# Gated linear attention and maxout FFN on one core: weights' conversion with one step less, joined output sums, turns' sums in four column tiles, and all lists written anew

## The chip, the core and the metric

One core of one Trainium2 chip runs the kernel. Its engines are TensorE (PE; the profile calls its weight loads PEld), VectorE (DVE), ScalarE (ACT), GpSimd (POOL) and SyncE (SP), which here only starts transfers. The metric is the device time of one execution in microseconds, the median of several runs.

## The reference

Two blocks follow each other. The first is a gated linear recurrence over 768 steps, for 4 batches of 8 heads with 48 features. The second is a maxout FFN over the 3072 tokens, from 384 features to 768 and back.

```python
mag = np.sqrt(a_re * a_re + a_im * a_im)
scale = np.minimum(mag, 0.999) / (mag + 1e-06)
a_re_n, a_im_n = (a_re * scale, a_im * scale)
for t in range(S):
    ar, ai = (a_re_n[:, :, t, :, None], a_im_n[:, :, t, :, None])
    new_re = ar * S_re - ai * S_im
    new_im = ar * S_im + ai * S_re
    kv = np.einsum('bhd,bhe->bhde', k[:, :, t], v[:, :, t])
    S_re, S_im = (new_re + kv, new_im)
    y[:, :, t] = np.einsum('bhd,bhde->bhe', q[:, :, t], S_re)
...
x = np.ascontiguousarray(attn_out.transpose(0, 2, 1, 3)).reshape(B * S, H * D)
h = np.maximum(np.maximum(x @ w1, x @ w2), x @ w3)
return (h @ w_out).astype(np.float32)
```

The four FFN weights arrive as 64-bit floats; all else is float32.

## The kernel before

**Tiling.** The tokens are cut into 12 groups, numbered 0 to 11; a group holds 128 steps of two batches, called x and y. The recurrence is computed by chunks: per group the gates' magnitude and angle, the sums of their logarithms and angles along the steps, and with these products inside a chunk and a state carried to the next.

**The list of words.** All work is written as words "name:group" in one string, SCHEDULE (line 21); `run` (line 955) does them one after the other. A last letter x or y names the batch, a 0 or 1 the batch in the early words of group 0. Each engine is wrapped in `Bound` (line 201), which ties each instruction behind the one issued before it on the same engine. So an engine works strictly in the order of the list, and waits where a word's inputs are not there. Because every call goes through `Bound`, all instructions bear its line, 210, in the profile. SLOTS (line 127) says which of four PSUM buffers of two banks each product gets; OTHER (line 134) names the words that run on the alternative engine, mostly DVE in place of ACT.

**The words that matter here.**

- `sqr`, `sqi`, `add`, `lnL`, `expe`, `expw`, `relu`, `lne`, `abs`, `xor`, `half`, `stt`, `atan`, `turn` turn the gates into logarithms (tiles Ln, L) and angles (tile w), on ACT and DVE.
- `cs` (line 586) sums the angles along the steps by a product with a triangle of ones, `upto`; per batch four matmuls, each with 64 columns of `upto`, so that two of them fill the array's columns. `t`, `nf`, `af`, `sa`, `sb` round the sums and take sine and cosine. `sums`, `F` and the `E` words do the like for the logarithms.
- `mk`, `mq`, `uk`, `uq` scale k and q (tiles k, q, uk, uq); `tpk`, `tpq` transpose them on PE into PSUM tile tp, and `Kc`, `Qc` copy that to tiles K and Q.
- `A` and `B` are the scores inside a chunk, `dk` the state's increment, `h` words carry the state (tile g), `y` is the block's output and `x` copies it to the FFN's features (tile xhx; xT in group 0). A, B and y use 32 columns of the array per matmul; sums, tp, dk and F use 64; the FFN's products use the whole array.
- `U` is the product with 768 x 384 blocks of a weight (PSUM tile up) and `u` the relu (first weight, folded into the others by `T`, `M`, `Wg`) or the running maximum. In group 0 they have shorter forms, and `O`, `o` are its output product.
- From group 1 on, the output product goes by seven half-size products, `P1` to `P7`, with `Px`, `Py` (PSUM tile op), and sums `S1` to `S4` (tile strassen) before and `r1`, `r6`, `r5`, `r7`, `r57`, `ox`, `oy` behind, which gather the result in tile ot. `D` stores it.
- `WL` loads one of 12 blocks of the weights as pairs of 32-bit words. `weight_step` (line 431) converts it to float32 into its place (tiles w and wo) through a scratch tile `ex` that lies in xhx: step `a` on ACT, `b`, `c`, `e`, `f` on DVE. The words of a pair are `low` and `high`, views that read every second word. The words are Wa, Wb and so on.

The loaded and intermediate tiles of the attention block come from pools with two buffers (`ldx`, `nat2`, `un2`, `fp2`).

Of the kernel before, what the change touches and what calls it, by code (L numbers as in the profile page):

```python
# [13 lines left out]
I32 = mybir.dt.int32  # L14
# [19 lines left out]
Bx:0 b0x:0 turn:1 b1x:0 h2x:0 mqx:1 Fx:1 f0x:1 We4:0 f1x:1 Wf4:0 f2x:1 add:2 csx:1 tx:1 yx:0 KBy:0 Q2y:0 nfx:1 xx:0
h3x:0 f3x:1 lnL:2 expe:2 Q1y:0 WL5:0 Wa5:0 Lkx:1 sumsy:1 csy:1 Eky:1 ty:1 Ay:0 kEny:0 Wb5:0 WL7:0 relu:2 mkx:1
g0y:0 Wc5:0 expw:2 U01x:0 nfy:1 abs:2 u01x:0 Lvy:1 We5:0 Eqy:1 Z2:0 g1y:0 Wa7:0 QBy:0 afy:1 Wf5:0 Eny:1 g2y:0 g3y:0
Wb7:0 Wg4:0 U11x:0 xor:2 By:0 dky:0 U02x:0 Lvx:1 b1y:0 h1y:0 b0y:0 QGy:0 yy:0 addw:2 lnw:2 expL:2 xy:0 U11y:0 Wg5:0
u02x:0 U02y:0 afx:1 half:2 u11x:0 Wc7:0 lne:2 We7:0 mulw:2 mulai:2 sbx:1 h2y:0 Z4:0 sax:1 h3y:0 stt:2 atan:2 Wf7:0
U12x:0 u12x:0 say:1 sby:1 Cdy:1 WL8:0 Cdx:1 turn:2 ukx:1 uqx:1 U01y:0 u01y:0 u11y:0 Wa8:0 U12y:0 csy:2 ty:2 u12y:0
csx:2 tpqx:1 tx:2 u02y:0 Qcx:1 nfy:2 Lnop:2 nfx:2 tpkx:1 Fy:1 kEnx:1 Wb8:0 Wc8:0 We8:0 Kcx:1 Wg7:0 Wf8:0 U21y:0  # L40
Wg8:0 KBx:1 f0y:1 u21y:0 Lky:1 Lqy:1 mky:1 afy:2 sumsx:2 dkx:1 Q1x:1 f1y:1 f2y:1 f3y:1 Enx:2 U21x:0 u21x:0 afx:2
U22y:0 u22y:0 Oy:0 Lqx:2 mqy:1 uky:1 uqy:1 tpqy:1 Ekx:2 Lix:3 Q2x:1 say:2 sby:2 sbx:2 sax:2 Eqx:2 h0x:1 h1x:1 QGx:1
h2x:1 oy:0 QBx:1 mkx:2 h3x:1 Qcy:1 Q1y:1 tpky:1 Kcy:1 Ax:1 g0x:1 Q2y:1 Liy:3 sqi:3 Fx:2 sumsy:2 g1x:1 g2x:1 U22x:0
Lrx:3 u22x:0 g3x:1 f3x:2 f2x:2 f1x:2 f0x:2 Lry:3 sqr:3 add:3 lnL:3 expe:3 Ay:1 relu:3 J3:0 g0y:1 g1y:1 mqx:2 g2y:1
Bx:1 KBy:1 kEny:1 lne:3 Ox:0 Eky:2 b1x:1 Eny:2 QBy:1 b0x:1 h0y:1 ukx:2 By:1 Eqy:2 yx:1 g3y:1 xx:1 b1y:1 Lqy:2 mqy:2
Lvx:2 ox:0 Lky:2 mky:2 b0y:1 tpkx:2 expw:3 Kcx:2 uqx:2 Lnop:3 uqy:2 tpqx:2 Qcx:2 QGy:1 dky:1 h1y:1 kEnx:2 sumsx:3
uky:2 Ekx:3 h2y:1 Eqx:3 Enx:3 yy:1 xy:1 Fy:2 f3y:2 h3y:1 dkx:2 f2y:2 abs:3 KBx:2 h0x:2 h1x:2 Q1x:2 f0y:2 f1y:2
U11:1 u11:1 tpky:2 Kcy:2 Lky:3 QBx:2 QGx:2 addw:3 Lqx:3 h2x:2 mqx:3 h3x:2 xor:3 half:3 Cdx:2 tpqy:2 Qcy:2 Q2x:2
lnw:3 kEny:2 expL:3 sumsy:3 Eqy:3 Q2y:2 Eny:3 Lkx:3 mkx:3 Fx:3 Eky:3 U01:1 Ax:2 Q1y:2 J1:0 mulw:3 mulai:3 g0x:2
g1x:2 u01:1 Cdy:2 f3x:3 f2x:3 g2x:2 g3x:2 J2:0 Bx:2 f0x:3 Dx:0 f1x:3 Dy:0 stt:3 KBy:2 h0x:3 U12:1 b0x:2 b1x:2 u12:1  # L50
S3:1 Lvy:2 yx:2 U02:1 QBy:2 Lvx:3 Lry:4 atan:3 turn:3 Liy:4 csy:3 csx:3 Lix:4 Lrx:4 sqr:4 sqi:4 add:4 lnL:4 ty:3
xx:2 By:2 u02:1 Ay:2 S1:1 nfy:3 relu:4 tx:3 expe:4 S2:1 expw:4 P5:1 P6:1 g0y:2 afy:3 say:3 sby:3 nfx:3 sbx:3 g1y:2
afx:3 sax:3 abs:4 dky:2 P1:1 Lqy:3 g2y:2 g3y:2 b1y:2 J4:0 QGy:2 P7:1 Px:1 P2:1 b0y:2 h0y:2 h1y:2 ukx:3 tpkx:3 lne:4
Lnop:4 r1:1 Liy:5 mky:3 h2y:2 h3y:2 S4:1 Kcx:3 uqx:3 yy:2 Lqx:4 kEnx:3 mqy:3 tpqx:3 Qcx:3 P3:1 r6:1 xy:2 Py:1 r5:1
r7:1 P4:1 Fy:3 uky:3 r57:1 f0y:3 f1y:3 xor:4 half:4 oy:1 ox:1 Q1x:3 addw:4 dkx:3 h1x:3 Lvy:3 f2y:3 f3y:3 h0y:3
h2x:3 sumsx:4 Ekx:4 h3x:3 lnw:4 QGx:3 expL:4 Eqx:4 Fx:4 KBx:3 U11:2 Dx:1 QBx:3 mulai:4 Q2x:3 f2x:4 Enx:4 u11:2
Cdy:3 Lkx:4 f1x:4 f0x:4 U01:2 uqy:3 f3x:4 mulw:4 stt:4 atan:4 tpky:3 Kcy:3 Ax:3 g0x:3 mqx:4 g1x:3 Bx:3 g2x:3 g3x:3
b1x:3 b0x:3 u01:2 Cdx:3 turn:4 U02:2 Lrx:5 u02:2 mkx:4 kEny:3 csy:4 csx:4 tx:4 nfx:4 ty:4 nfy:4 yx:3 xx:3 sumsy:4
KBy:3 Eqy:4 Eky:4 Lry:5 S3:2 Eny:4 sqr:5 dky:3 h1y:3 h2y:3 h3y:3 tpqy:3 Qcy:3 Q2y:3 Lix:5 sqi:5 Px:2 afy:4 add:5
lnL:5 expe:5 Dy:1 U12:2 u12:2 S1:2 Py:2 P7:2 Q1y:3 relu:5 lne:5 QBy:3 afx:4 P4:2 Ay:3 By:3 expw:5 S2:2 g0y:3 sbx:4  # L60
abs:5 g1y:3 sax:4 QGy:3 ukx:4 uqx:4 P6:2 P5:2 S4:2 g2y:3 g3y:3 P2:2 P1:2 Lqy:4 r1:2 Liy:6 mqy:4 b1y:3 P3:2 b0y:3
r6:2 r5:2 r7:2 tpkx:4 r57:2 ox:2 oy:2 kEnx:4 tpqx:4 yy:3 xy:3 Fy:4 say:4 Lky:4 sby:4 mky:4 uky:4 Lnop:5 Kcx:4 uqy:4
sumsx:5 xor:5 half:5 U11:3 KBx:4 addw:5 lnw:5 expL:5 mulw:5 Lqx:5 mulai:5 Cdx:4 h0x:4 f2y:4 stt:5 f3y:4 Ekx:5 f0y:4
Lkx:5 Dy:2 Dx:2 Qcx:4 Enx:5 Q1x:4 Cdy:4 u11:3 Eqx:5 QBx:4 mkx:5 Lry:6 QGx:4 Lvx:4 U01:3 Lix:6 atan:5 Q2x:4 u01:3
f1y:4 h0y:4 U02:3 Lrx:6 u02:3 sqr:6 dkx:4 h1x:4 sqi:6 h2x:4 h3x:4 Fx:5 f0x:5 f3x:5 add:6 f1x:5 f2x:5 Ax:4 g0x:4
Lqy:5 g1x:4 Bx:4 lnL:6 expe:6 g2x:4 g3x:4 U12:3 lne:6 b1x:4 tpky:4 turn:5 mqx:5 b0x:4 tpqy:4 Qcy:4 u12:3 Lvy:4
kEny:4 S1:3 csy:5 ty:5 csx:5 Kcy:4 dky:4 nfy:5 S3:3 sumsy:5 h1y:4 h2y:4 tx:5 nfx:5 h3y:4 afy:5 yx:4 Eky:5 Eny:5
Eqy:5 afx:5 Q2y:4 Q1y:4 sbx:5 P5:3 P1:3 P7:3 Lky:5 sax:5 Ay:4 xx:4 KBy:4 ukx:5 uqx:5 Lrx:7 tpqx:5 S2:3 expw:6
relu:6 QBy:4 Lnop:6 mky:5 tpkx:5 S4:3 Kcx:5 g0y:4 Qcx:5 P6:3 Px:3 Py:3 r1:3 By:4 P2:3 P4:3 say:5 sby:5 QGy:4 g1y:4
abs:6 g2y:4 g3y:4 b1y:4 b0y:4 KBx:5 mqy:5 r6:3 r5:3 r7:3 r57:3 kEnx:5 oy:3 Q1x:5 uky:5 xor:6 Lry:7 sqr:7 Fy:5 f2y:5  # L70
sumsx:6 uqy:5 f3y:5 yy:4 P3:3 ox:3 f0y:5 Lkx:6 xy:4 QGx:5 addw:6 U11:4 Liy:7 Dx:3 QBx:5 Ekx:6 mkx:6 Enx:6 Lvx:5
f1y:5 lnw:6 Lqx:6 h0y:5 u11:4 Q2x:5 expL:6 mulai:6 mulw:6 U01:4 u01:4 tpky:5 h0x:5 Eqx:6 Kcy:5 tpqy:5 stt:6 Ax:5
Lix:7 atan:6 g0x:5 Qcy:5 g1x:5 g2x:5 Bx:5 kEny:5 g3x:5 b0x:5 Q2y:5 U02:4 sqi:7 b1x:5 add:7 lnL:7 relu:7 expe:7
u02:4 U12:4 Fx:6 f2x:6 S3:4 f3x:6 half:6 turn:6 f0x:6 u12:4 Lvy:5 dky:5 h1y:5 Q1y:5 f1x:6 sumsy:6 dkx:5 Eny:6 csy:6
csx:6 h1x:5 mqx:6 S1:4 Dy:3 ty:6 nfy:6 S2:4 Eqy:6 Lqy:6 mqy:6 Eky:6 P1:4 KBy:5 tx:6 nfx:6 afx:6 lne:7 expw:7 afy:6
P7:4 abs:7 Lky:6 Ay:5 QBy:5 g0y:5 g1y:5 g2y:5 yx:5 g3y:5 addw:7 sbx:6 sax:6 ukx:6 uqx:6 By:5 say:6 P5:4 xx:5 P6:4
r1:4 r6:4 r5:4 lnw:7 xor:7 S4:4 half:7 Px:4 P2:4 b0y:5 Py:4 r7:4 P4:4 r57:4 P3:4 expL:7 mulw:7 QGy:5 oy:4 tpqx:6
tpkx:6 b1y:5 Lnop:7 mky:6 Qcx:6 Q1x:6 ox:4 Liy:8 kEnx:6 yy:5 sumsx:7 xy:5 Cdx:6 Enx:7 Fy:6 f2y:6 f0y:6 f3y:6
mulai:7 f1y:6 Eqx:7 QBx:6 QGx:6 Q2x:6 stt:7 Lqx:7 Ekx:7 Lix:8 U01:5 sqi:8 Lry:8 Cdy:6 Kcx:6 Lrx:8 Lvx:6 dkx:6 h1x:6
sby:6 mqx:7 h2x:6 h3x:6 uqy:6 uky:6 sqr:8 add:8 Dy:4 atan:7 turn:7 Ax:6 g0x:6 lnL:8 Lkx:7 expe:8 xor:8 g1x:6 relu:8  # L80
# [962 lines left out]
```

## Time and profile before

| what | value |
|---|---|
| runs | 558.76, 561.72, 562.83 us; median 561.72 us |
| span of the profiled execution | 556.9 us |
| mean granted clock of TensorE | 0.988 |
| first matmul of PE | after 10.46 us |
| instructions | 22739 |

The profile is of one execution, and the span goes from its first instruction to its last; the time of a run holds in addition what lies around that, so the median is 4.8 us above the span. Busy times are sums over an engine's instructions. Matmuls overlap each other, so the mean duration of a matmul is longer than the step from one to the next.

### The profile page before, as it was taken

The page shows a single profiled execution, that of the slowest core. Times are in us where ns is not written, and L with a number is a line of the kernel's source. Part 1 is how long each engine was busy: PE and PEld are TensorE (multiplying, and loading weights), DVE is VectorE, ACT ScalarE, POOL GpSimd, SP SyncE. Part 2 cuts the span into 40 slices and gives each one's busy share as a digit, 9 for nine tenths or more (in the row PEclk, how much of TensorE's full clock was granted, in tenths as well). Part 3 has the DMA queues.
Part 4 walks back from the last instruction along what each step waited for, and adds up shares of the span by engine and source line. Part 5 has one row for each costly group of instructions (what it writes and reads, how often), then busy time and mean ns, then how long its engine had stood idle before and what let it go on. Part 6 is the DMA issues. An engine that isn't in the chain of part 4 may idle for free.

```text
span 556.9 us, 22739 instructions
## 1 busy us (share of the span) xinstructions
PE 524.6 (94%) x10086; PEld 449.0 (81%) x10086; DVE 490.4 (88%) x770; ACT 370.0 (66%) x652; POOL 74.4 (13%) x117
## 2 busy tenths in 40 slices
PE   1669799989999999999999999999999999999997
PEld 0356588778888898888988888988888888998986
DVE  5999999989998899999988897999999999886524
ACT  5999989867965867787766858777646855530100
POOL 8105250002030001000120200120010020000000
PEclk9869999999999999999999999999999999999999
DMA  8977976456055164235364136542361144000000
GB/s 218 287 191 156 206 154 102 78 105 123 18 108 109 21 123 77 48 63 92 68 115 82 33 61 121 110 88 50 58 126 31 32 88 82 10 31 2 7 25 29
DMA packets 142530, 49.09 MB, mean 88 GB/s; under 512 B 130528, under 2 KB 135648, under 8 KB 142432
## 3 DMA queue, kind: packets, MB, share of 16 engines
q1 hardware_dynamic: 136272, 37.77, 31.9%
q0 software_dynamic: 6160, 9.87, 10.4%
q8 instruction: 79, 1.29, 1.0%
q14 instruction: 19, 0.16, 0.1%
HBM read 33.03 MB, written 4.72 MB: 68 GB/s over the span
## 4 chain that ended last, share of the span: by engine, by line
PE 84%; DVE 6%; DMA 4%; SPq 2%; issue 1%; ACT 1%; POOL 0%; DVEq 0%
PE up L210 34%; PE op L210 24%; PE y L210 7%; PE A L210 5%; PE tp L210 4%; PE dk L210 4%; PE sums L210 3%; PE cs L210 2%; SPq L210 2%; DMA xhx<-in_moe_w_out_dram 2%; PE F L210 2%; DVE xhx L210 1%; PE B L210 1%; DMA k<-in_k_dram 1%; DMA ar<-nf 1%
## 5 line engine op out<-in xcount | busy, mean ns | idle before, releaser
L210 PE MATMUL up<-xhx,w 128*128 128x256 f32 x792 | 177.4, 382 | 0.1
L210 PEld LDWEIGHTS up<-xhx,w 128*128 128x128 f32 x792 | 148.6, 190 | 21.5 <-PE B L210 0.3
L210 ACT ACT_TABLE_LOAD x45 | 57.7, 1283 | 1.5 <-PEq L1027 0.8
L210 ACT COPY atm<-B 32x128 f32<-32x128 f32 x96 | 24.5, 255 | 36.9 <-DVE atm L210 22.9
L210 PE MATMUL op<-wo,xhx 128*128 128x192 f32 (+1 forms) x220 | 48.5, 364 | 0.0
L210 DVE TENSOR_TENSOR Q<-Q,f 112x1024 f32<-112x1024 f32 (+1 forms) x48 | 45.4, 950 | 0.8 <-ACT Q L210 0.6
L210 ACT ACTIVATE f<-F 48x232 f32<-48x232 f32 x96 | 34.4, 359 | 13.2 <-PE F L210 5.4
L210 POOL DMA_DIRECT2D ar<-nf x40 | 34.2, 1280 | 65.3 <-DVE ar L210 54.7
L210 PE MATMUL y<-atm,vb 128*32 128x64 f32 x1152 | 39.4, 221 | 1.4 <-issue 1.1
L210 PEld LDWEIGHTS op<-wo,xhx 128*128 128x128 f32 x220 | 36.5, 190 | 4.3 <-DVE q L210 0.3
L210 POOL DMA_DIRECT2D Ln<-e x11 | 11.1, 1005 | 214.6 <-ACT e L210 53.9
L210 PE MATMUL y<-QG,g 112*32 112x64 f32 x1408 | 38.4, 219 | 0.9 <-issue 0.8
L210 PEld LDWEIGHTS y<-atm,vb 128*32 128x32 f32 x1152 | 32.5, 109 | 6.4 <-issue 3.6
L210 PEld LDWEIGHTS y<-QG,g 112*32 112x32 f32 x1408 | 34.8, 109 | 1.3 <-issue 1.0
L210 DVE TENSOR_TENSOR ot<-ot,op 128x192 f32<-128x192 f32 (+1 forms) x67 | 27.1, 413 | 9.0 <-PE op L210 4.3
L210 PE MATMUL op<-wo,strassen 128*128 128x192 f32 x176 | 33.0, 331 | 0.0
L210 PE MATMUL A<-Q,K 112*32 112x80 f32 x1536 | 31.6, 234 | 1.3 <-DVE Q L210 1.3
L210 DVE COPY_PREDICATED atm<-masko,A 128x256 f32<-128x256 uint8 x72 | 31.2, 435 | 1.6
L210 PE MATMUL op<-w,strassen 128*128 128x192 f32 x176 | 32.5, 329 | 0.0
L210 PEld LDWEIGHTS A<-Q,K 112*32 112x32 f32 x1536 | 27.2, 110 | 5.0 <-issue 1.9
L210 ACT COPY Q<-tp 112x1024 f32<-112x1024 f32 x23 | 23.3, 1013 | 10.3 <-PE tp L210 10.0
L210 ACT COPY ot<-op 128x192 f32<-128x192 f32 (+1 forms) x13 | 4.5, 342 | 38.2 <-PE op L210 38.2
(151 smaller groups left out, 1120.8 us busy)
## 6 DMA issues: line engine op xcount, KB each, us to landing
ar<-in_a_re_dram SPq DMA_DIRECT2D x24, 192.0 KB, 3.7
ai<-in_a_im_dram SPq DMA_DIRECT2D x24, 192.0 KB, 3.8
q<-in_q_dram SPq DMA_DIRECT2D x96, 48.0 KB, 2.6
k<-in_k_dram SPq DMA_DIRECT2D x96, 48.0 KB, 2.9
vb<-in_v_dram SPq DMA_DIRECT2D x96, 48.0 KB, 3.1
out_dram<-ot SPq DMA_DIRECT2D x23, 192.0 KB, 2.8
Ln<-e POOLq DMA_DIRECT2D x11, 384.0 KB, 4.7
w<-L POOLq DMA_DIRECT2D x9, 384.0 KB, 4.7
```

Of the source, the lines that this page charges most:

```text
L210: ins = f(*a, **kw)
```

## The change

The diff has six parts.

1. **Weights' conversion.** The sign is kept through the conversion: step b now clips `high` from both sides and writes the scratch tile, a scales it in place with a function that treats the signs differently, c shifts, and e joins the low bits and writes the weight's place. Step f goes, and the sign bit is no longer masked and put back. The order is b, a, c, e.
2. **Output sums.** r5 and r7 become one addition, r75, over the middle half of a joined tile for both batches.
3. **Turns' sums in quarters.** `cs` makes eight matmuls of 32 columns in place of four of 64, per batch.
4. **Constants.** Biases of ACT are given as numbers and no longer read from tile `biases`, which keeps one column of ones.
5. **Fixed tiles.** The pools `ldx`, `nat2`, `un2`, `fp2` go; k, q, t, nf, af, CS, Ln, E, K, Q and ot are fixed tiles, one for each batch or for odd and even groups. Ek and Eq get tiles of their own.
6. **Lists.** SCHEDULE, SLOTS and OTHER are all new. The whole-array products are spread otherwise over the list. Among the words of OTHER (on DVE): Qc six times, before once; Kc four, before seven; the relu of u ten, before six; af eleven, before eight; x three, before five; relu of the logarithms three, before four.

```diff
-        if step == "a":
-            activation(out=ex.bitcast(FP), in_=high.bitcast(FP), func=AF.Abs, scale=2.0 ** -112)
-        elif step == "b":
-            dve.tensor_single_scalar(out=ex.bitcast(FP), in_=ex.bitcast(FP), scalar=LAST, op=OP.min)
+        if step == "b":
+            dve.tensor_scalar(out=ex.bitcast(FP), in0=high.bitcast(FP), scalar1=LAST, scalar2=-LAST, op0=OP.min,
+                              op1=OP.max)
+        elif step == "a":
+            activation(out=ex.bitcast(FP), in_=ex.bitcast(FP), func=AF.Prelu, alpha=-2.0 ** 32,
+                       scale=-2.0 ** -112 if i in (0, 3, 6) else 2.0 ** -112)
         elif step == "c":
-            if i in (0, 3, 6):
-                dve.tensor_scalar(out=ex, in0=ex, scalar1=3, scalar2=-0x80000000, op0=OP.logical_shift_left,
-                                  op1=OP.bitwise_or)
-            else:
-                dve.tensor_single_scalar(out=ex, in_=ex, scalar=3, op=OP.logical_shift_left)
+            dve.tensor_single_scalar(out=ex, in_=ex, scalar=3, op=OP.logical_shift_left)
         elif step == "e":
-            dve.scalar_tensor_tensor(out=ex, in0=low, scalar=29, in1=ex, op0=OP.logical_shift_right, op1=OP.bitwise_or)
-        elif step == "f":
-            dve.scalar_tensor_tensor(out=dst.bitcast(I32), in0=high, scalar=-0x80000000, in1=ex,
-                                     op0=OP.bitwise_and, op1=OP.bitwise_xor)
+            dve.scalar_tensor_tensor(out=dst.bitcast(I32), in0=low, scalar=29, in1=ex, op0=OP.logical_shift_right,
+                                     op1=OP.bitwise_or)
...
             for ch in range(2):
-                for j in range(2):
-                    dst, m = ps[j * L64:(j + 1) * L64, ch * HC:(ch + 1) * HC], slice(ch * L64, (ch + 1) * L64)
-                    mm(out=dst, lhsT=upto[:, m], rhs=every(T["w", g][:, c * DM:(c + 1) * DM], j), start=True, stop=True)
+                for o in (0, L64, 32, L64 + 32):
+                    j, m = o // L64, slice(ch * L64 + o % L64, ch * L64 + o % L64 + 32)
+                    mm(out=ps[o:o + 32, ch * HC:(ch + 1) * HC], lhsT=upto[:, m],
+                       rhs=every(T["w", g][:, c * DM:(c + 1) * DM], j), start=True, stop=True)
...
-                activation(out=e, in_=e, func=AF.Ln, scale=1e-6 * math.exp(-LNMAX), bias=least)
+                activation(out=e, in_=e, func=AF.Ln, scale=1e-6 * math.exp(-LNMAX), bias=math.exp(-LNMAX))
...
-                out, in0, in1 = {"r6": (yl, xl, r.get(6)), "r5": (xr, yl, r.get(5)), "r7": (yl, yl, r.get(7)),
-                                 "r57": (yr, yl, r.get(5)), "ox": (ot[0], ot[0], ps[:, 0, 0:DM]),
-                                 "oy": (ot[1], ot[1], ps[:, 1, 0:DM])}[name]
+                if name == "r75":
+                    two_ = ot.rearrange("p c n -> p (c n)")[:, NH:3 * NH].rearrange("p (u n) -> p u n", u=2)
+                    again = yl.rearrange("p (u n) -> p u n", u=1).to_broadcast([P, 2, NH])
+                    dve.tensor_tensor(out=two_, in0=again, in1=ps[:, 1, 0:DM].rearrange("p (u n) -> p u n", u=2), op=OP.add)
+                    return
+                out, in0, in1 = {"r6": (yl, xl, r.get(6)), "r57": (yr, yl, r.get(5)),
+                                 "ox": (ot[:, 0], ot[:, 0], ps[:, 0, 0:DM]),
+                                 "oy": (ot[:, 1], ot[:, 1], ps[:, 1, 0:DM])}[name]
```

More of the change, by code (lines that the diff above doesn't have):

```diff
@@ L62 @@
[L62 to L66, printed above, removed]
@@ L72 @@
[L72 to L76, printed above, removed]
@@ L77 @@
[L77 to L80, printed above, removed]
-g2x:6 mkx:7 U11:5 KBx:6 u11:5 g3x:6 U12:5 u01:5 lne:8 U02:5 u12:5 S3:5 Lnop:8 u02:5 Bx:6 b0x:6 b1x:6 tpky:6 tpqy:6
@@ L922, in seven @@
         else:
-            ot = [once(("ot", g * C + c), lambda: fp2.tile([P, DM], FP, tag="ot", name="ot")) for c in range(C)]
-            xl, xr, yl, yr = (ot[c][:, h * NH:(h + 1) * NH] for c in range(C) for h in range(2))
+            ot = ots
+            xl, xr, yl, yr = (ot[:, c, h * NH:(h + 1) * NH] for c in range(C) for h in range(2))
             if name == "r1":
```

254 lines of the change are left out of this document (133 added, 121 removed).

## The prediction

> **What bounds the kernel now.** I read the page first, then the busy time by stretches, then what TensorE (PE) waited for, then single rows.
>
> ```profile
> span 556.9 us, 22739 instructions
> ...
> PE 524.6 (94%) x10086; PEld 449.0 (81%) x10086; DVE 490.4 (88%) x770; ACT 370.0 (66%) x652; POOL 74.4 (13%) x117
> ...
> q8 instruction: 79, 1.29, 1.0%
> ...
> PE 84%; DVE 6%; DMA 4%; SPq 2%; issue 1%; ACT 1%; POOL 0%; DVEq 0%
> ```
>
> PE is busy 94% of the span and makes up 84% of the chain that ended last. DVE, at 88%, is close behind. The average hides two stages, which the stretches show:
>
> ```profile
> 20.00:40.00 20.00, 10.83 (x112) 7.62 (x104) 19.93 (x31) 19.80 (x33) 0.00 (x0) 0.66 0.88 220
> 40.00:60.00 20.00, 19.35 (x283) 12.19 (x282) 19.93 (x30) 18.92 (x28) 10.40 (x13) 1.00 0.79 169
> 60.00:80.00 20.00, 16.12 (x415) 13.78 (x416) 19.86 (x32) 18.06 (x37) 7.54 (x9) 1.00 0.89 182
> 90.00:557.00 467.00, 460.60 (x9032) 402.85 (x9024) 407.69 (x636) 290.51 (x514) 40.91 (x49) 1.00 0.35 67
> ```
>
> The columns are the stretch, its length, the busy time of PE, PEld, DVE, ACT and POOL, the granted clock, the DMA share and GB/s. From 20 to 80 us DVE works 19.9 of every 20 us and PE has gaps: this stage converts the weights and starts group 0, and DVE sets its end. From 90 us on PE works 460.60 of 467 us, the 6.4 us left containing the last add and store: here only PE's own time counts, and DVE has 59 us to spare. The waits of PE agree:
>
> ```profile
> PE pw L210 <- ACT w L210: 10.5, 1, 10.5
> PE cs L210 <- DVE w L210: 4.5, 2, 3.2
> PE tp L210 <- DVE uq L210: 2.6, 3, 1.7
> PE y L210 <- issue: 1.9, 2, 1.1
> ```
>
> The first three lie almost wholly in the first 90 us. The fourth, time in which PE waited for nothing that the profile shows, lies in the dense part. So three things can move the end: how far PE is behind its own work when it becomes dense, PE's own time after that, and these "issue" stalls.
>
> **PE's own time: changes of tile shape.**
>
> ```profile
> 143.72 1.52 PE L210 MATMUL cs<-w,upto 128*64 128x192 f32 x16
> 145.17 0.46 PE L210 MATMUL B<-QB,KB 112*32 112x32 f32 x32
> 145.44 1.33 PE L210 MATMUL A<-Q,K 112*32 112x80 f32 x64
> 146.71 0.43 PE L210 MATMUL op<-wo,strassen 128*128 128x192 f32 x1
> ```
>
> ```profile
> L210 PE MATMUL A<-Q,K 112*32 112x80 f32 x1216 | 25.0, 234 | 0.0
> ...
> L210 PE MATMUL cs<-w,upto 128*64 128x192 f32 x144 | 13.7, 332 | 0.0
> ...
> L210 PE MATMUL B<-QB,KB 112*32 112x32 f32 x608 | 8.9, 198 | 0.0
> ```
>
> A merged row ends one matmul's duration after its last start. The last cs began at 143.72 + 1.52 - 0.332 = 144.91. The 16 go in pairs (two column tiles of 64 at once), so a pair takes (144.91 - 143.72) / 7 = 0.17 us and the next could have begun at 145.08; B, which has 32-column tiles, began at 145.17, 0.09 later. The last A began at 145.44 + 1.33 - 0.234 = 146.54; its quads of four 32-column tiles come every 1.096 / 15.75 = 0.07 us; op, whole-array, began at 146.71, again 0.10 late. From B to A, both with 32-column tiles, nothing is lost: the last B began at 145.17 + 0.46 - 0.198 = 145.43, the first A at 145.44. So a change of tile shape costs about 0.095 us. Counted along PE's instruction lists, there are 190 such changes before and 149 after: 21 fewer by the new order, then 20 by cs taking the 32-column shape. 41 x 0.095 = 3.9 us. Of them 30 come after the first whole up product of group 1, where PE is dense (2.85 us, safe); the other 11 (1.05 us) lie ahead of it, where part may turn into waiting for DVE.
>
> The quartered cs itself: 96 calls become 192, each with half the rows of result and the same 192 columns, four at once instead of two. By A's quads the four share the time of one, so I take a cs word at the same 8 steps, cost 0. Bounds: below 0 nothing, as the 192 streamed columns stay; above, if the four tiles ran as two pairs, 1.36 us for 0.68, 24 x 0.68 = +16 us. I take 0 because A is the row of that very shape. The Trainium skill ("TensorEngine Tiling (Array Packing)", Instruction Overhead) says that each matmul carries some 60 cycles of overhead, which speaks against more and smaller matmuls; A's 64 start every 1.096 / 63 = 17 ns for 80 columns each, so the trace shows that it isn't paid one after the other where tiles alternate.
>
> **The startup: DVE.**
>
> ```profile
> L210 DVE TENSOR_TENSOR ot<-ot,op 128x192 f32<-128x192 f32 x46 | 16.1, 351 | 5.9 <-ACT ot L210 3.7 <-PE op L210 1.3
> ...
> L210 DVE TENSOR_TENSOR ot<-ot,op 128x384 f32<-128x384 f32 x21 | 11.1, 549 | 3.1 <-PE op L210 3.0
> L210 DVE SCALAR_TENSOR_TENSOR w<-w,ar 128x768 f32<-128x768 f32 x11 | 10.5, 952 | 1.9 <-ACT w L210 1.8
> ...
> L210 DVE COPY K<-tp 112x1024 f32<-112x1024 f32 x7 | 8.6, 1222 | 1.6 <-PE tp L210 1.6
> ...
> L210 DVE TENSOR_SCALAR xhx<-xhx 128x768 f32<-128x768 f32 x12 | 7.5, 621 | 2.8 <-ACT xhx L210 2.7
> ...
> L210 DVE TENSOR_SCALAR xhx<-up 128x768 f32<-128x768 f32 x6 | 5.7, 954 | 11.5 <-PE up L210 11.5
> L210 DVE SCALAR_TENSOR_TENSOR xhx<-w,xhx 128x768 int32<-128x768 int32 x4 | 3.8, 955 | 0.1
> ```
>
> Twelve blocks each lose step f: 12 x 0.955 = 11.5 us of DVE. Step b changes from a minimum over packed words (0.621) to minimum and maximum over every second word. That form isn't in the trace. Below: 0.621, one source and packed output. Above: 0.955, the row that also reads every second word and has two sources. I take 0.65, nearer to the row of the same operation, so +0.3 us; the upper end makes it +4.0. Net 11.2 (7.5 to 11.5) us less, all in the stage that DVE sets. The Trainium skill ("Vector Engine (DVE) Microarchitecture Reference", The SBUF access granule) says that a source stepping word by word without adjacent pairs streams some 1.7 times slower, which would put b near 1.4 us by estimate; the trace disagrees for this step of two words: 955 ns for the stepping source against 952 for the packed one (w<-w,ar).
>
> Little of the 11.2 arrives at PE. The new conversion goes DVE, ACT, DVE (b, then Prelu, then c), where it went ACT, DVE; a is now behind DVE's b, and c and e behind ACT again. And everything else is listed anew. So I walked both lists by hand: every word at its row's duration, starting when its engine's last word and its producers are done, b at 0.65. The walk of before was fitted to the trace; after has DVE start about 2.5 us later against its own work (loads arrive when they did). What counts is PE's lag: the time of a word less PE's own work and shape changes ahead of it.
>
> ```profile
> 118.82 0.22 PE L210 MATMUL y<-QG,g 112*32 112x64 f32 x1
> 120.16 0.24 PE L210 MATMUL y<-atm,vb 128*32 128x64 f32 x1 [1.12 <-issue]
> ...
> 121.93 0.48 PE L210 MATMUL up<-xhx,w 128*128 128x256 f32 x1
> ```
>
> Before, the first whole up product of group 1 begins at 121.93 with 78.7 us of PE's work and 45 changes (4.3 us) ahead of it: lag 38.9. After, by the walk, it begins at 116.2 with 78.5 us and 34 changes (3.2) ahead: lag 34.5, so 4.4 less. Some 16 us later, at the first cs of group 3, PE waits about 2 us for DVE's turn, and the gain is 2.8 (39.1 against 36.3). From there DVE has room as before. I take the middle, 3.6 us, and 2.8 to 4.4 as bounds at this b. With b at 0.955 the walk gives back about 2.6 us (not all 3.7, since ACT and loads end some waits), so the low end is 0.2.
>
> **After the startup, DVE and ACT.** Joining r5 and r7 into one 128x384 add saves 11 x (2 x 0.351 - 0.549) = 1.7 us of DVE. Four more relus on DVE cost 4 x 0.954 = 3.8, five more copies of Q less three of K 2 x 1.222 = 2.4; the other moves (three af, two y, one Ln) nearly cancel. Net +4.5 us on an engine with 59 us to spare: nothing, unless a chain ends on it. ACT (66%) loses what DVE takes, and its biases become constants: nothing. Pools turned into fixed tiles keep two buffers each, one per half of a group: nothing, and the freed Ek/Eq tile can only lift a wait. At the end both lists close with an output product, ox or oy and the store: nothing.
>
> **Issue stalls.** The stop before 120.16 comes at an instruction of PE whose number is a multiple of 256, counting from a fixed start; so do the three others in the dense part. q8 fetched 79 packets of 16 KB (1.29 MB / 79), and (10086 matmuls + 10086 weight loads) / 79 = 255: one packet is a line of 256 instructions. The fetched line can be late where 256 instructions run shorter than a fetch. With PE's time for each 256 summed from the rows, the three lines under 3.8 us after the startup fall short of it by 2.8 us in all, and the stalls found come to 2.2: 3.8 us fits as the time of a fetch. After has eight such lines, 3.65 us short in all, though the two worst (2.4 and 2.6 us) become 2.8 and 2.9. Scaled, 2.9 us of stalls, 0.7 more. The announced spreading of the whole-array products leaves 3 lines without one, where there were 6, but makes more lines middling short.
>
> **Sum.** 3.9 + 3.6 - 0.7 = 6.8 us off the span, which would be 550.1. The median of the runs, 561.72, is 4.8 above the span and takes the same: 554.9, say 555.
>
> **The rivals.**
>
> *No change, about 559.5.* Step b costs 0.955, and at the first cs of group 3 or a little later the turns' wait eats the rest: startup 0.2, or less. 3.9 + 0.2 - 0.7 = 3.4 gives 558.3; with 2 us more of such waits 560.3. For it: DVE is at 99% for 60 us, and my walk has ideal hand-overs among three engines. Against: the stepping rows cost no more than packed ones. By the skill's rule for adjacent pairs (b at 1.4) the loss would be 12 x 0.75 x 0.7 (2.6 / 3.7) = 6.3 us against my sum, 561.2: this same case.
>
> *Slower, about 568.* A fetch takes longer than 3.8 us. Then the many middling lines all stall: at 5.0 us after's lines are short by 25.3 us and before's by 11.2, so 14.1 more, less 3.9 + 3.6 gives 561.7 + 6.6 = 568. It decides from about 4.6 us, where the difference reaches 7.5. For it: 20 lines under 4.5 us against 6. Against: before would itself have to show 6.5 us of stalls at 4.5, and shows 2.2; only lines crowded by transfers could be that late. The same side has quarters of cs that run in pairs: 561.7 - 6.8 + 16 = 571.
>
> *More gain, about 551.* b packs as well as before, the wait at group 3's cs doesn't come (4.4 us at the startup), and breaking up the two worst lines ends the stalls (+2.2): 3.9 + 4.4 + 2.2 = 10.5, 551.2.
>
> That the change doesn't do what it says holds for one part: the lists still leave three lines without a whole-array product.
>
> **Chances.** Forecast 0.42 (552 to 558), no change 0.28, slower 0.17, more gain 0.13. A gain over 1%, about what can be told from no change, needs less than 556.1: all of the last, three quarters of the first, 0.13 + 0.32 = 0.45. Within 1%: the rest of the forecast and the no-change case, 0.38. Slower 0.17. For 8 in 10 the range goes from 550 to 564.5, with the forecast's own at 552 to 558.
>
> **What would show it.** Each cs word still takes about 0.66 us with the next 32-column product following at once; b's row between 0.62 and 0.66; PE at group 1's first up product near 116 us; PE busy from 90 us on with less than 3 us of "issue"; span near 550. Wrong if cs takes 1.3 us, if b's row is at 0.95 or over, if PE waits on DVE's w or uq after 120 us by more than 3 us, or if "issue" grows past 5.

## The result and the profile after

| | before | after |
|---|---|---|
| median of the runs | 561.19 us (4 runs, 558.76 to 562.83) | 596.31 us (4 runs, 592.76 to 597.80) |
| span of the profiled execution | 556.9 us | 594.6 us |
| mean granted clock of TensorE | 0.988 | 0.966 |

The ratio is 1.062, with a 95% interval of 1.056 to 1.068. The kernel became 35 us slower, far outside the range. The profiled execution of after took 596.25 us, 1.7 above its span. Its counterpart of before fits the fastest of the runs, 558.76, which is 1.9 above its span, so of the 4.8 us that the part before the prediction puts between median and span, some 3 are the choice of that execution.

First the page of after, then the stretches (columns as in the prediction), then what PE waited for (us in all, times, longest).

```profile
span 594.6 us, 23062 instructions
...
PE 536.4 (90%) x10278; PEld 458.0 (77%) x10278; DVE 480.6 (81%) x751; ACT 360.9 (61%) x646; POOL 75.0 (13%) x117
...
PEclk9759899999999999999799999999999799999999
...
q8 instruction: 81, 1.33, 0.9%
...
PE 62%; DVE 10%; issue 9%; DMA 7%; SPq 6%; ACT 3%; POOL 1%; DVEq 0%; ACTq 0%; POOLq 0%
```

```profile
20.00:40.00 20.00, 13.12 (x252) 10.22 (x252) 18.23 (x30) 18.43 (x30) 0.00 (x0) 0.62 0.94 221
40.00:60.00 20.00, 18.08 (x108) 10.44 (x108) 18.85 (x29) 16.82 (x27) 8.47 (x8) 0.87 0.91 186
60.00:80.00 20.00, 15.95 (x464) 14.25 (x464) 14.79 (x25) 14.52 (x29) 7.33 (x11) 0.91 0.86 183
90.00:594.60 504.60, 470.82 (x9308) 409.13 (x9300) 406.76 (x628) 289.62 (x517) 41.49 (x49) 0.98 0.32 62
```

```profile
PE op L201 <- ACT ot L201: 11.4, 4, 5.3
...
PE wt L201 <- DVE w L201: 5.0, 1, 5.0
PE y L201 <- issue: 4.6, 4, 1.9
PE tp L201 <- DVE nf L201: 3.2, 1, 3.2
PE dk L201 <- DMA vb<-in_v_dram: 2.3, 2, 1.5
PE sums L201 <- issue: 2.1, 2, 1.1
```

DVE and ACT do less work than before and POOL about the same. DVE in the startup, full before, has slack now (18.23, 18.85 and 14.79 of 20 us), and still the startup isn't shorter, so DVE alone doesn't set it. Hand-overs between engines are one candidate. The DMA engines are another, busy 0.94 and 0.91 from 20 to 60 us (0.88 and 0.79 before), and no run separates the two. The chain of waits has changed with it: PE's share falls from 84% to 62%, and DVE, "issue", DMA and SP's queue fill in. From 90 us on PE stands still for 504.60 - 470.82 = 33.8 us, against 6.4 before; both hold some 3.6 us behind the last matmul. The largest cause, 11.4 us at the output products, has no counterpart in the waits of before.

**Where the 37.7 us of the spans lie.** The first whole up product of group 1 begins at 124.54 us instead of 121.93: 2.6 us. From there to the end it is 470.1 us against 435.0: 35.1 more. In that part PE's gaps add up to 27.9 us (ACT 12.9, issue 7.1, DVE 5.4, loads 2.3), before to 1.1 (issue 0.9): 26.8 more. If the shape changes saved their 2.85 there, some 11 us remain as slower running.

The granted clock explains about half of that. The row of clock tenths above has a 7 at slices 19 and 31 (counted from 0). The clock's own records put three stretches at half speed behind group 1: from 236.43 for 3.4 us, from 287.62 for 6.8 and from 465.12 for 6.8. PE works 3.4, 3.8 and 4.7 us in them; the rest of them is gaps, which are counted already. Work at half speed loses half its time, so the clock costs 11.9 / 2 = 6.0 us. Before, it is 1.00 everywhere after 40 us. The other 5 us or so stay unexplained.

One such place close up, by stretches of 2 us:

```profile
284.00:286.00 2.00, 1.36 (x8) 1.06 (x7) 2.00 (x4) 1.84 (x4) 0.00 (x0) 1.00 0.64 121
286.00:288.00 2.00, 0.00 (x0) 0.00 (x0) 2.00 (x5) 1.49 (x2) 0.00 (x0) 0.91 0.32 53
288.00:290.00 2.00, 0.00 (x0) 0.00 (x0) 0.27 (x2) 0.00 (x0) 0.00 (x0) 0.50 0.67 158
290.00:292.00 2.00, 1.32 (x4) 1.32 (x5) 1.08 (x3) 1.67 (x3) 0.00 (x0) 0.50 0.77 141
292.00:294.00 2.00, 2.00 (x7) 1.74 (x6) 0.00 (x0) 1.94 (x5) 0.00 (x0) 0.50 0.26 45
294.00:296.00 2.00, 2.00 (x11) 1.76 (x10) 0.00 (x0) 1.96 (x4) 0.00 (x0) 0.89 0.00 0
```

PE stops at 285.4, and the mean of 0.91 from 286 to 288 puts the clock's fall to half at 287.64, 2.3 us into the gap (2 x 0.09 / 0.5 = 0.36 us ahead of 288). PE resumes at 290.68 and works at half speed until 294.44 by the same sum, 3.8 us. So a gap of 5.3 us costs nearly 2 us more than its length. The Trainium skill ("TensorE: Matmul & The Clock Gate", Part 1) says that the clock falls to half after an idle window of about 3.4 us, placed freely, and recovers after about as long a busy one. The trace agrees on the return, 3.8 us of work, but not on the idle window: here the clock fell 2.3 us into the gap, and at 236.43 it fell behind two shorter ones.

```profile
234.59 0.29 PE L201 MATMUL dk<-vb,uk 64*64 64x48 f32 x4 [0.79 <-DMA vb<-in_v_dram]
236.42 1.83 PE L201 MATMUL dk<-vb,uk 64*64 64x48 f32 x59 [1.53 <-DMA vb<-in_v_dram]
```

In the 3.4 us ahead of these two falls PE had worked 1.1 us each time. So short stops that follow each other closely cost the clock here too.

The timeline of after shows what PE waited for in three places (start, length, engine, operation; in brackets the idle time before and what ended it):

```profile
57.04 0.89 SPq L201 DMA_DIRECT2D strassen<-in_moe_w_dram  x1
63.19 0.56 DVE L201 TENSOR_SCALAR xhx<-strassen 128x768 f32<-128x768 f32 x1 [3.36 <-DMA strassen<-in_moe_w_dram]
65.14 0.66 PE L201 MATMUL tp<-ident,uq 64*112 64x64 f32 x16 [3.17 <-DVE nf L201]
...
264.06 2.63 SPq L201 DMA_DIRECT2D q<-in_q_dram  x4
288.02 0.55 SPq L201 DMA_DIRECT2D out_dram<-ot  x1
290.31 0.32 ACT L201 COPY ot<-op 128x192 f32<-128x192 f32 x1 [2.81 <-DMA out_dram<-ot]
290.68 2.61 PE L201 MATMUL op<-w,strassen 128*128 128x192 f32 x7 [5.33 <-ACT ot L201]
...
423.03 0.24 PE L201 MATMUL y<-atm,vb 128*32 128x64 f32 x1 [1.88 <-issue]
```

Read the middle group from the bottom. PE waits 5.33 us at P6:4 for the copy r1:4 on ACT, which shares a PSUM tile with it. ACT waits 2.81 us in r1:4, because tile ot may only be overwritten when it has been stored. SP starts that store at 288.02, although the last addition into ot was done by 263.2: from 264.06 SP had started 31 loads in a row, most of them 0.66 us apart (2.63 us for four), with some 4.5 us between them in which SP waited for PE to free a load's tile, and the store stands behind them in the list. The other two places are a conversion that waited for its late-queued load (top) and a stop at a line end (bottom), the place where PE passes from one fetched line of 256 instructions to the next.

### The profile page after: what moved, and what is told of

Same layout as the page of the kernel before. It is cut to its first block, busy times and chain, and to the rows that moved or that the text cites. A ratio compares the mean times of both kernels' runs of the same rounds, so it can differ in the third digit from the quotient of the medians.

```text
span 594.6 us, 23062 instructions
## 1 busy us (share of the span) xinstructions
PE 536.4 (90%) x10278; PEld 458.0 (77%) x10278; DVE 480.6 (81%) x751; ACT 360.9 (61%) x646; POOL 75.0 (13%) x117
## 3 DMA queue, kind: packets, MB, share of 16 engines
q8 instruction: 81, 1.33, 0.9%
## 4 chain that ended last, share of the span: by engine, by line
PE 62%; DVE 10%; issue 9%; DMA 7%; SPq 6%; ACT 3%; POOL 1%; DVEq 0%; ACTq 0%; POOLq 0%
PE up L201 25%; PE op L201 16%; SPq L201 6%; PE y L201 5%; PE A L201 3%; PE tp L201 3%; PE dk L201 3%; PE sums L201 2%; PE cs L201 2%; DMA strassen<-in_moe_w_dram 2%; DVE w L201 2%; DMA w<-L 1%; PE F L201 1%; DVE ot L201 1%; DVE xhx L201 1%
## 5 line engine op out<-in xcount | busy, mean ns | idle before, releaser
L201 DVE TENSOR_TENSOR ot<-ot,op 128x384 f32<-128x384 f32 (+1 forms) x56 | 25.6, 465 | 33.2 <-issue 13.4
L201 PE MATMUL op<-wo,xhx 128*128 128x192 f32 (+1 forms) x220 | 50.2, 367 | 1.5 <-DVE ot L201 1.3
L201 POOL DMA_DIRECT2D ar<-nf x40 | 37.6, 1359 | 95.4 <-DVE ar L201 76.5
L201 DVE TENSOR_TENSOR Q<-Q,f 112x512 f32<-112x512 f32 (+1 forms) x48 | 45.0, 952 | 2.9 <-ACT f L201 1.7
L201 PE MATMUL op<-w,strassen 128*128 128x192 f32 x176 | 35.1, 348 | 5.9 <-ACT ot L201 5.7
L201 PEld LDWEIGHTS op<-w,strassen 128*128 128x128 f32 x176 | 31.1, 203 | 7.6 <-ACT ot L201 6.3
L201 PEld LDWEIGHTS op<-wo,strassen 128*128 128x128 f32 x176 | 30.1, 196 | 8.4 <-ACT ot L201 6.1
L201 ACT COPY Q<-tp 112x1024 f32<-112x1024 f32 x18 | 18.2, 1011 | 27.4 <-PE tp L201 27.3
L201 DVE TENSOR_TENSOR xhx<-xhx,up 128x768 f32<-128x768 f32 x22 | 20.9, 951 | 14.9 <-PE up L201 14.6
```

Of the source, the lines that this page charges most:

```text
L201: ins = f(*a, **kw)
```

## The experiments

Each version is timed beside the kernel before on the same chip; "behind group 1" means from that group's first whole up product on. They are told by question: which part costs the time (1 to 4), what makes the waits at the output products (5 to 11), the waits removed only where they occur (12), and two controls (13 and 14). Experiments 2, 3 and 13 test whether the line ends set PE's "issue" stops.

**1. All the code with the lists of before.** Parts 1 to 5 of the change, and SCHEDULE, SLOTS and OTHER from before, with r75 for r5 and r7 and the conversion's words in the new order. The values differ from the reference's; the likely reason is that before's order overwrites fixed tiles ahead of their last reading, which no run here shows.

```diff
-SCHEDULE = (after's)
+SCHEDULE = (before's; Wb Wa Wc We for Wa Wb Wc We Wf; r75 for r5, r7)
```

> The lists of before (SCHEDULE, SLOTS, OTHER) with all the other parts of the change: the new conversion (Wb at Wa's old place and Wa at Wb's, We at Wf's), r75 at the later place of r5 and r7, cs in quarters, constant biases, fixed tiles. Theory L, the new lists cost the time and the other parts do not: 553 to 560 us, somewhat under before's 561, DVE busy some 8 to 12 us less. Theory P, one of the other parts is slow (the clipping read of every second word, the quarters, the fixed tiles): over 575 us.

Measured: 582.67 us against 558.52, ratio 1.039 (1.034 to 1.045). The code alone costs 24 us in the old lists, so the new lists aren't the only loss; with them the same code takes 14 us more. The two don't simply add up, since each list was made for its own code. Behind group 1 PE stands still for 10.0 us, 8.2 of them issue; another 7.4 us of issue lie in the startup.

**2. Only the quarters**, in the kernel before.

```diff
-                for j in range(2):
+                for o in (0, L64, 32, L64 + 32):
...
```

> The kernel before with cs in quarters and nothing else changed: 384 more instructions on PE, 16 more with every cs word. Theory F, the lists are laid out for the places at which PE's lines of 256 instructions end, and shifting these places costs stalls: summed over before's trace with the shifted ends, lines fall short of 3.5 to 3.8 us by 20 to 26 us where they fall short by 1 to 2 now; the run with all other parts showed 15 us of issue waits. So 573 to 582 us. Rival, the quarters only save 8 changes of tile shape: 557 to 561.

Measured: 571.50 against 561.97, 1.021 (1.015 to 1.027). From 90 us on, in an execution of 575.75 us:

```profile
90.00:573.00 483.00, 467.88 (x9280) 407.09 (x9275) 411.79 (x641) 293.93 (x519) 40.89 (x49) 1.00 0.35 66
```

483.00 - 467.88 = 15.1 us idle at a clock of 1.00, and 0.8 more up to the span's end, where before had 6.4; 8.4 of the 8.6 us of gaps behind group 1 are issue. The row of cs itself costs nothing more (see below). What costs, by experiment 3, is that 192 more matmuls and as many weight loads, 384 instructions, move every later end of a 256-instruction line in the list.

**3. Only the places of the line ends**, in the kernel before: 24 small matmuls at the start, each 4 instructions of PE, whose product isn't used.

```diff
+    pad = psum.tile([P, 2, 512], FP, tag="ps6", name="pad")
+    for _ in range(24):
+        mm(out=pad[:, 0, 0:4], lhsT=upto, rhs=upto[:, 0:4], start=True, stop=True)
```

> The kernel before with 24 small matmuls (96 instructions of PE, result not used) ahead of its first product, in time in which PE waits anyway. Nothing else differs, so no work is added where PE is dense; only the ends of the lines of 256 instructions move by 96. Theory F: lines fall short of 3.5 to 3.8 us by 25 to 32 us, 578 to 590 us, with issue waits of some 20 us. Rival, fetches are early enough wherever the ends lie and e1 was slow for another reason: 558 to 563.

Measured: 587.94 against 561.97, 1.049 (1.042 to 1.057). The stretch and three waits:

```profile
90.00:583.00 493.00, 470.08 (x9151) 409.60 (x9146) 412.17 (x641) 294.47 (x519) 40.90 (x49) 1.00 0.34 65
```

```profile
PE B L210 <- issue: 4.8, 4, 1.6
PE dk L210 <- issue: 4.4, 5, 1.7
PE F L210 <- issue: 4.2, 4, 1.8
```

Twenty-four matmuls of four columns cost 26 us, because 96 instructions shift the line ends into stretches of short matmuls (B, dk, F); issue behind group 1 goes from 0.9 to 16.1 us. Of the 26.5 us by the spans, 20.2 lie behind group 1, 15.2 of them issue. The order of before suits its own line ends; of other places only these two were tried, and both cost time.

The traces of all versions show the place itself. In the 20 traces there are 180 issue stops of PE over 0.15 us. Counted over PE's recorded instructions from 0, 177 of them stand at the same place in every 256 (remainder 193 or 194), and each time PE resumes 1.2 to 1.6 us after the end of a packet of q8. The other three lie in the startups of experiments 1 and 4.

**4. Only the conversion**, in the kernel before: its words in the order b, a, c, e, with f dropped, and the steps' code as in the diff.

> The kernel before with the new conversion of the weights and nothing else (PE's instructions are the same): Wb at Wa's place, Wa at Wb's, We at Wf's. Theory C, the 12 steps saved on DVE help while DVE sets the end: 553 to 558 us. Rival D, DVE now starts each block itself and waits for its load and then for ACT, and the saving is lost there: 559 to 564.

Measured: 568.03 against 561.97, 1.013 (1.007 to 1.019). Less work on DVE makes that list slower, by more than either theory gave: group 1's first whole up product begins at 132.6 us instead of 121.9, and behind it there are only 0.7 us of gaps. Ahead of it PE's gaps are 34.6 us instead of 27.6, and of the 7.0 more, 5.8 are issue, though PE's instructions are the same: other timing makes other line ends late. The opposite edit, the old steps in after's list (Abs at Wb's place, the minimum at Wa's, e and f both at We's), stands against it.

> The changed kernel with the old steps of the conversion at the new list's places: Abs on ACT at Wb's, the minimum on DVE at Wa's, c as before, e and f one behind the other at We's. All else as changed. Theory D, the new conversion's DVE-ACT-DVE order costs more than the step saved, as in e7 (6 us): 586 to 592 us. Rival C, the new list is laid out for the new conversion, which saves 11 us of DVE there: 598 to 606.

Measured: 612.91 against 561.10, 1.095 (1.088 to 1.103), 16.6 us above after. One stop of 7.8 us, at 47.5 us, is part of it:

```profile
45.39 0.56 DVE L201 TENSOR_SCALAR xhx<-xhx 128x768 f32<-128x768 f32 x1 [3.53 <-ACT xhx L201]
46.47 0.95 DVE L201 TENSOR_TENSOR uk<-uk,En 128x768 f32<-128x768 f32 x1
47.52 1.95 PE L201 MATMUL dk<-vb,uk 64*64 64x48 f32 x64 [7.80 <-issue]
```

The profile names "issue", but this stop is at no line end, and dk reads the tile uk, whose scaling on DVE ended at 46.47 + 0.95 = 47.42. DVE had stood 3.53 us at the old step b, which waited for the old step a on ACT. So the old steps' hand-over explains a good part of the stop, and each list is slower with the other's steps.

**5. The stores earlier.** In after, each D word right behind the addition that completes its half of ot.

```diff
- ... h0x:4 ox:2 ... tpqx:4 oy:2 ... Lnop:6 Lkx:5 Dy:2 Lvx:5 Lky:5 Dx:2
+ ... h0x:4 ox:2 Dx:2 ... tpqx:4 oy:2 Dy:2 ... Lnop:6 Lkx:5 Lvx:5 Lky:5
```

> The changed kernel with only its 22 store words (Dx, Dy of groups 1 to 11) moved: each stands right behind its last addition (ox, oy), ahead of the loads that stood before it on SP. Theory S, the stores wait in SP's queue behind loads, r1 of the next group waits for the store, and PE for r1: the waits of op for ot (11.4 us) and the slow clock after the long ones (about 5 us) go, 578 to 584 us. Theory F, the time goes to fetches and to waits spread over the new order: 592 to 597, since the store's wait is replaced by the next one.

Measured: 594.81 against 558.52, 1.063 (1.056 to 1.071), as after. P6:4 still waits, for the reason behind the first:

```profile
289.98 0.30 ACT L201 COPY ot<-op 128x192 f32<-128x192 f32 x1
290.34 2.93 PE L201 MATMUL op<-w,strassen 128*128 128x192 f32 x8 [3.10 <-ACT ot L201]
```

The store no longer holds r1:4, but ACT comes to it only at 289.98, behind the exponentials of group 6, a table load and a sine, which stand ahead of it in the list.

**6. All of SP's words by release**: stores as in 5, and each load right behind the last reading of the tile that it overwrites.

> As the kernel with early stores, and the loads of k, q, v (groups 2, or 4, on) and of the gates (groups 6 on) stand right behind the word that frees their tile, and the load of weight block 7 right behind that of block 5. Theory S, SP's order is the cause of most of the loss: 565 to 575 us, the waits for v and k and DVE's 3.4 us wait at block 7 gone as well. Theory F: over 585.

Measured: 593.50 against 558.52, 1.059 (1.053 to 1.065): a few us at most.

**7. The load of weight block 7 earlier**, behind that of block 5.

```diff
- ... WL5:0 Lvy:0 Lkx:1 Wb5:0 mqy:0 turn:1 KBx:0 WL7:0 Wa5:0
+ ... WL5:0 WL7:0 Lvy:0 Lkx:1 Wb5:0 mqy:0 turn:1 KBx:0 Wa5:0
```

> The changed kernel with one word moved: the load of weight block 7 right behind that of block 5, ahead of eight loads of v and k. Theory S: DVE's wait of 3.4 us at block 7's first step goes and PE's wait of 3.2 us for uq at 65 us goes with it; 592 to 594 us, 2 to 4 less than the changed kernel. Rival, DVE is late there anyway by its own work: no difference.

Measured: 595.19 against 558.52, 1.063 (1.056 to 1.069). DVE's wait at block 7 falls from 3.4 to 0.5 us and the time stays, so that wait alone doesn't set it.

**8. r1 later in all groups**: behind the last of P1, P5, P6, P7, so that no product stands behind the copy.

```diff
-Eqx:6 sby:6 r1:4 sax:6 expL:7 P6:4 Px:4 P2:4 P5:4 P7:4 g3y:5
+Eqx:6 sby:6 sax:6 expL:7 P6:4 Px:4 P2:4 P5:4 P7:4 r1:4 g3y:5
```

> The changed kernel with the 11 words r1 moved behind the last of P1, P5, P6, P7 of their group, as before had it in most groups. Theory R, PE's waits of op for ot (11.4 us) come from r1's place: products into the same PSUM tile wait for r1, which stands behind table loads and a store on ACT; with them goes the slow clock after the long ones (about 5 us): 578 to 585 us. Rival, the next product waits for something else as late: 590 to 597.

Measured: 601.00 against 561.97, 1.073 (1.065 to 1.080): slower than after. The waits of this version behind 121 us:

```profile
PE sums L201 <- ACT xhx L201: 4.1, 1, 4.1
PE op L201 <- DVE strassen L201: 3.6, 2, 2.2
PE A L201 <- ACT atm L201: 3.2, 1, 3.2
```

The 11.4 us of "op <- ACT ot" are gone. But PE had waited so in four places only, and the new waits are for work that stands behind r1 on ACT.

**9. No table loads**: Arctan and Sin replaced by Exp, in after and in before, so the angles are not the reference's.

```diff
-            activation(out=w, in_=w, func=AF.Arctan)
+            activation(out=w, in_=w, func=AF.Exp)
...
```

> The changed kernel with sine and arctangent replaced by the exponential, so that ACT needs no other function table: 44 of its 45 table loads go, 56 us of ACT's 361, and the angles are not the reference's. PE's and DVE's instructions are the same. Theory A, the waits of PE for ACT behind group 1 (12.9 us) and the slow clock that follows them (8 us) come from ACT's order, with the table loads ahead of what PE needs: 568 to 580 us. Rival B, as in e2 and e8 another wait takes the place: 587 to 596.

> The same replacement in the kernel before, as a measure of what ACT's table loads are worth where PE waits for ACT only in the startup: behind group 1 PE waits 0.1 us for ACT. Theory A and B: 552 to 560, what is gained is gained ahead of 122 us.

Measured: after 596.78 against 561.10, 1.067 (1.061 to 1.072); before 557.91, 0.998 (0.994 to 1.003). In after ACT is busy 303.6 us instead of 360.9, and neither kernel's time moves. The wait at P6:4 shows why:

```profile
291.27 0.32 ACT L201 COPY ot<-op 128x192 f32<-128x192 f32 x1 [3.07 <-DMA out_dram<-ot]
291.64 2.93 PE L201 MATMUL op<-w,strassen 128*128 128x192 f32 x8 [4.37 <-ACT ot L201]
```

An emptier ACT arrives at r1:4 earlier and waits there for the same store.

**10 and 11. Several removals together.** Since 5 and 9 each left the other's wait, r1 late in all groups was combined with the early stores, with SP's words by release, and with both SP's order and no table loads (the angles again not the reference's).

> The changed kernel with both moves: stores right behind their last addition (as e2) and r1 behind the last of P1, P5, P6, P7 (as e8). Theory T, two late chains stand in parallel at the same places (r1 waits for the store, and PE for r1; moved back alone, r1 holds up ACT's later copies until the store is done): the pair gains what neither did alone, 575 to 587 us. Rival L, the new order is short of slack everywhere and the next wait comes: 591 to 602.

> As e12, and the loads of k, q, v and of the gates by release with block 7 behind block 5 (as e3). Theory T: 4 to 8 us less than e12, the waits for v gone as well. Rival L: within 3 us of e12.

> As e13, and sine and arctangent as the exponential (as e10), so that ACT has 56 us less of table loads; the angles are not the reference's. Theory A, ACT's order is late in parallel with SP's queue and r1's place, and all three together set PE's waits: 562 to 575 us. Rival L, what is left are waits for DVE and for fetches and the slow clock behind them: over 583.

Measured, against 561.76: 597.64, 1.069 (1.059 to 1.079); 596.84, 1.065 (1.058 to 1.073); 593.98, 1.059 (1.053 to 1.066). The waits of 8 remain (A for atm 3.2 us in all three), and by release the load of v comes late (dk waits 4.0). Edits in every group make about as much waiting as they remove.

**12. Only where the trace shows the wait.** r1 late only in groups 1, 4 and 8; each store behind its addition; the load Lvx:4 ahead of Lvx:5; block 7's load behind block 5's.

> The changed kernel with moves only at the places where PE was seen to wait: r1 behind the last of P1, P5, P6, P7 in groups 1, 4 and 8 alone, stores right behind their last addition, the load of v for x of group 4 ahead of that of group 5, weight block 7 right behind block 5. Theory T, each wait has its own cause, and e8 and e12 to e14 gained nothing because r1 moved in all groups (and all loads moved) made new waits in groups 2, 3, 7 and 9: the waits at 156, 235, 291 and 467 us go with their slow clock, 1.5 + 4.2 + 7.4 + 6.8, and 1 to 3 us at block 7: 573 to 581 us. Rival L, the next wait comes at each place: over 588.

Measured: 577.87 against 560.12, 1.032 (1.024 to 1.040): 18.4 us below after's 596.31.

```profile
90.00:577.00 487.00, 466.57 (x9323) 404.87 (x9321) 406.91 (x628) 290.64 (x519) 41.27 (x49) 1.00 0.34 64
```

```profile
PE sums L201 <- issue: 2.5, 3, 1.5
PE op L201 <- DVE strassen L201: 1.8, 2, 1.4
PE op L201 <- ACT ot L201: 0.4, 1, 0.4
```

Idle from 90 us on falls from 33.8 to 21.3 us (20.4 in the stretch shown and 0.9 behind it), the waits for ot from 11.4 to 0.4, and the clock behind 100 us is 1.00 throughout; the longest gap behind group 1 is 1.57 us. From group 1's up product to the end it takes 18.4 us less than after, which 12.7 us less of gaps and 6.0 of the clock account for. So the four moves together take away half of the loss. They weren't tried one by one; by the gaps it is the waits for r1 in three groups and the load of v, with the slow clock behind them. Behind group 1 remain issue 6.9, DVE 6.6 and ACT 1.6 us.

**13. The line ends in the targeted version**: 2 and 12 small matmuls at the start, 8 and 48 instructions.

> The targeted version with 2 small matmuls (8 PE instructions) ahead of everything, so that every later line of 256 instructions ends 8 instructions earlier in the list; their product is not used. With the trace of the targeted version and 3.8 us for a fetch, the lines fall short of it by 3.1 us in all as they are and by 0.5 us with the 8. Theory F (the new list still pays for the places of its line ends, within a few instructions): the stalls without a shown cause behind the startup fall from 6.9 to 2 to 4 us, time 572 to 576. Theory N (such stalls come from crowded transfers or chance, not from the places): 6 us of them or more, time 576 to 581.

> The same with 12 small matmuls, 48 PE instructions. By the same sum the lines fall 19.5 us short. Where 96 instructions were put ahead of the kernel before, 32.3 us short by the sum came with 20 us of stalls and 26 us of time, so theory F: 12 to 16 us of stalls behind the startup, time 586 to 598. Theory N: 576 to 581, as with 8.

Measured, against 560.19: 581.56, 1.037 (1.030 to 1.043), and 591.48, 1.055 (1.048 to 1.062). Behind 125 us, issue is 8.9 us with 8 instructions, where 2 to 4 were expected, and 16.3 with 48, where 12 to 16 were. The new list too depends on its line ends, by 10 us and more for 48 instructions. But the sum of short lines isn't good to a few instructions: with 8 neither the stops nor the time fell.

**14. Constant biases alone**, in the kernel before.

```diff
-    hpi, lnmax, least = (biases[:, i:i + 1] for i in range(3))
+    hpi, lnmax, least = -0.5 * math.pi, LNMAX, math.exp(-LNMAX)
```

> The kernel before with ACT's biases as numbers and one memset in place of three, nothing else: 38 ACT instructions some 0.095 us shorter, PE's instructions the same. Behind group 1 PE waits for ACT 0.1 us, so 558 to 562 us by the theory that this part of the change is worth nothing; a part worth keeping would show 557 or less.

Measured: 559.16 against 560.12, 1.000 (0.996 to 1.004). Nothing, as predicted. The joined addition and the fixed tiles weren't tried alone. No version was found that beats the kernel before.

## Why the prediction was wrong

**Changes of tile shape, 3.9 us: size not contradicted, but lost.** The rows of after:

```profile
398.23 1.51 PE L201 MATMUL cs<-w,upto 128*32 128x192 f32 x32
399.56 1.29 PE L201 MATMUL A<-Q,K 112*32 112x80 f32 x64
```

32 quarters, two words, take 1.33 us up to the start of the next 32-column product: 0.66 for a word, as expected. Before, two words took 143.72 to 145.17, 1.45 us, with one change. The rival of quarters in pairs (1.36 a word) falls. The gain would lie in PE's own time, where no run shows it apart from the rest, and the waits are ten times larger.

**Step b: right.** The grouped rows of DVE:

```profile
L201 DVE TENSOR_SCALAR xhx<-xhx 128x768 f32<-128x768 f32 x4 | 2.5, 616 | 0.7 <-DMA xhx<-in_moe_w_dram 0.7
L201 DVE TENSOR_SCALAR xhx<-w 128x768 f32<-128x768 f32 x4 | 2.4, 607 | 0.4 <-DMA w<-in_moe_w_dram 0.4
L201 DVE TENSOR_SCALAR xhx<-strassen 128x768 f32<-128x768 f32 x3 | 1.7, 561 | 3.8 <-DMA strassen<-in_moe_w_dram 3.8
```

561 to 616 ns, no more than the packed form, so the rule for adjacent pairs that the prediction took from the Trainium skill ("Vector Engine (DVE) Microarchitecture Reference", The SBUF access granule) doesn't hold for this step of two words.

**The startup, 3.6 us gained: this step failed too.** The walk gave group 1's up product at 116.2 us; it came at 124.54, with a lag of 42.8 us instead of 34.5 (before 38.9). The walk let "loads arrive when they did" and made hand-overs among three engines ideal. In the trace, weight loads stand behind other starts on SP (57.04), DVE waits 3.8 us in that row of b for them, and the clock is slower (0.62, 0.87 and 0.91 by stretch, before 0.66, 1.00, 1.00). PE's gaps in the startup add up to 26.7 us against 27.6 before, so it isn't more waiting. It is slower running: by the clock's records PE works 18.7 us of the startup at half speed, against 8.5 before, which costs some 5 us more.

The size of this loss is open, since the startup varies between executions: in that of experiment 14, with before's list, the same product came at 128.34 us. But no trace of the new list has it ahead of 123.3 us (experiment 7), so the gain wasn't there. Experiment 4 shows that the shorter conversion isn't a gain by itself.

**"DVE and ACT after the startup: nothing, unless a chain ends on it": this step failed most.** It priced slack as an average, 59 us of DVE and a third of ACT. But the lists are new, and a list with slack can have a copy at the wrong place: 11.4 us at four products that stood behind r1. SP's words weren't walked at all, though SP is one queue at 0.66 us a start. Experiment 12 shows this step's share: 18 us, with the clock.

**Issue, 2.9 us expected.** It measured 7.1 behind group 1, 7.6 in all, past the 5 that the prediction had given as a sign of being wrong. The rival named the mechanism, a fetch longer than 3.8 us, but not its size (14.1 more). At the nine such stops of after over 0.15 us, 3.9 to 7.0 us (median 5.2) go by from PE's crossing into a line until it resumes in the next: the packet starts 1.3 to 4.8 us after the crossing, takes 0.9 to 1.3, and PE resumes 1.25 to 1.6 after its end. At the 22 stops of experiment 3 it is 3.0 to 5.2 us (median 3.5). There is no one threshold, so the error was to take 3.8 us from the few short stops of before, whose order suited its line ends.

**The rivals.** "No change", "more gain" and the pairs fall. The one on the slower side was right in its sign, and its mechanism is a part of the loss, in the trace of after the smaller one. The larger part, new single waits behind group 1 and the slow clock after them, was no rival and had no price.

**What stays open.** The targeted version is still 17.8 us slower, 21.0 by the spans. Its trace has 14.1 us more gaps behind group 1 than before and reaches group 1's up product 4.4 us later (126.3); no run removed these. Why a packet starts up to 4.8 us late isn't settled. With the DMA engines over half busy the median start in the trace of after is 1.3 us behind the crossing, with under a tenth 0.8, but starts near 4.8 occur with both. Why the conversion is slower in the old list (experiment 4) was read from one startup. And some 5 us of slower running behind group 1, which neither gaps nor clock show, have no cause here.

## What to carry to other kernels

Where an order is written out, a rewritten order is itself the change: walk each queue, the one that only starts transfers too, and ask at each copy that frees a buffer what stands behind it, since slack as an average hides single waits. A change that adds instructions to PE moves every later line end, so price it by the lines it moves and not by its own work; in a fitted order 96 instructions cost 26 us. When a wait is to be removed, move the word only in the groups where the trace shows it, and count the slow clock behind a gap, but only for the work done in it (2.3 us to the fall and 3.8 to the return here; two stops of 0.79 and 1.53 us did it as well).

## What was not expected of the hardware

The price of a line end's place was larger than all arithmetic in the change: +9.5 us for 192 more matmuls that take no time of their own. The time between crossing a line and the start of the next packet varies: 1.3 to 4.8 us at the stops of after, 0.4 to 2.8 at those of experiment 3. The clock fell with PE working 1.1 of the 3.4 us ahead, and not only behind a long stop. And a step of two words on a single source costs DVE nothing: 561 to 616 ns, against 621 packed.
